# A convolution by Fourier transforms with its gradients: the inverse transforms' first step over halves of the array's rows, and state sums of two exponents at a time

## The chip, the core and the metric

The kernel runs on one core of a Trainium2 chip. The core has TensorE (PE, matrix products; PEld in the profile is its loading of weights), VectorE (DVE), ScalarE (ACT), GpSimd (POOL) and SyncE (SP, which here only issues DMAs). The engines run side by side, each works through its own queue in order, and semaphores tie them together. Products are written to PSUM, from which VectorE or ScalarE must copy them to SBUF; such a copy is called an evacuation below. The metric is the device time of one execution in microseconds, lower is better.

## What is computed

A layer's forward pass and all its gradients. The forward pass, cut to its core:

```python
xn = layernorm(x)                                    # 2048 rows of 512 channels, bf16
P  = exp(dt*A * l)                                   # per channel 128 complex states, l = 0..2047
K  = real(einsum("dn,dnl,dn->dl", C, P, dt*B))       # one convolution kernel per channel
s  = irfft(rfft(xn, 4096) * rfft(K, 4096))[:2048] + xn * Dskip
g  = silu(silu(xn @ w1) @ w2)                        # w1 512 x 1792, w2 1792 x 512
out = x + s * g
```

Beside `out` the kernel returns the gradients of x, A, B, C (real and imaginary parts), log_dt, Dskip, w1 and w2 for a given gradient of `out`.

## The kernel before

**Transforms.** A transform of 4096 points is done by products with small tables, in blocks of 128 channels. Forward (`dft_fwd`): a first step with the table TF (L405), transposes (L415), and a second step with F2 (L425); F2 has 64 columns, and its products are written alternately to the lower and the upper 64 PSUM partitions. Inverse (`dft_inv`): a first step with the spectrum Y as the stationary operand and the table I2 as the moving one (L440), then a second with TI (L453). In the first step there are 16 groups of 128 spectrum rows, and each group takes a product for the real and one for the imaginary part, 128 rows by 256 columns, both added into the same part of PSUM. Four groups are one set: eight products, then one evacuation (the `ev` call behind them), which sorts the values into A2. A set fills two PSUM banks. I2 holds a twiddle table times a mask: row p of a group meets only those 8 of the 128 columns' places that belong to it, and the mask is built in `gen_step_tables` from the row's number (`pg`, `e8`). There are 12 inverse transforms: one for each of four blocks in the forward convolution (stream C, `gen_conv_fwd`), two for each block in the backward one (stream B, `gen_conv_bwd`).

**State gradients.** The kernel's gradient is folded (`gen_ssm_fold`) and multiplied by the powers of the state matrix (`gen_ssm_v`, L998, evacuated to Vb). VectorE multiplies Vb with the table E (`gen_ssm_products`, L1013, to Tp): real and imaginary products for each of 21 exponents. `gen_ssm_sums` adds them up over the exponents on TensorE, by products with the identity matrix, in the PSUM tile psS: three rows of 64 values a partition. It does so for 16 groups, four for each block of channels; ScalarE copies each group's psS into Sa (L1037). `gen_ssm_grads` starts by subtracting the third row of Sa from the first (L1072), and goes on to the parameters' gradients.

**Order.** All instructions are issued in an order written out by hand or by a planner. Every part of the work is a generator, and every `yield` ends a step. PLAN is a string with a letter for each step: `play` takes the letters in order and advances the named generator. PLAN has seven sections, parted by `/`; between them memory pools are closed and opened. Since each engine's queue is in order, PLAN is the order of every queue, SP's and POOL's DMAs included. WAYS says for each evacuation of a stream whether ScalarE (A) or VectorE (D) does it. SLOTS says which buffer of a rotating set each tile takes. Streams named below: 0 to 8 and p are the setup (7 the magnitudes, ScalarE exponentials at L508; 6 the layer norm; 5 the step tables); J, F the forward dense pass (L751, L768); P, Q, R the tables and the convolution kernels; X, C the forward convolution; D, B the backward one; d, A, x the backward dense pass (L1149, L1169); N, Y, V, T, S, Z the state gradients; h, t, w and g, v the gradients of the dense weights (L1202, L1231); i, k, m the layer norm's gradient.

Section 2 of PLAN (counted from 1) holds the forward convolution with the forward dense pass, section 4 the backward convolution with the backward dense pass, section 5 the state gradients' start with the last of the backward dense pass, section 6 the state gradients with the dense weights' gradients.

Of the kernel before, what the change touches and what calls it, by code (L numbers as in the profile page):

```python
# [39 lines left out]
AAAAAAYAAAAAANNxVVVVAAxVVVVVVAATTVVxxVVxVVYxVVTYYxxxxNNNTTTTNSVVVVVVVYxSx/VTTSTSVTTVVVVVhhVVVSSVVVVVVVTTTYYttTtSthVTTNTT  # L40
tttYwwtSVVVVSgVVVVtStthVtNNwNNwNVTwTTVVVwwNNNNZZTgStZSZZVtVVwVZtZtYYYhgvvYvvVZTTTTVVwVwZZVZVVSVVVVVYtTSTTTVvvwVttVVSVVVV
TTTvSTwgVVVhVVSYvtZZttwYYTTVThTVZtVVvZvZtVVVVVTSvvhVVVVSVVtSwwVVvVwTTTTwtTYYYVVVVZSSVTVVVZTTYtZZttZtvtVVVSVtTSVVVVvvVTgT
TZYZYTTwTVVVZZwvVVVZVZZVZhwwwSwStghtVVggVVSStwZgvVVZZVVhTTTvZZZTvTvTTSvvTvtSSStttvgthZvvwwttZZttZgZwwwZhZZZZvZvZZtttwwt/
wttivtiikkhvkwwikktkmkkmkkkmttmmmkimmvgkvvviigvvvvvwwkkmvttvkkkkwwvvkmkwkgmwwwkkimmkkmkmvmkmmmvvvvvvvvvmvkkkkmmmvmvvvvvv
# [5 lines left out]
fp.XT=01010101;pf.pf=012010210210210210210210210210210210210210210120120120120120121210210120120120120201202102102102102  # L50
102102102102102021020202012012021020210212012010120120120120202012012012012012012012012012020102121021021021021201201201
2012012010101020120101202;fp.hT=0101010101010101;fp.ob=0101010;dft.w8=01231032013123032120132021032103;pc.pc=01010101010
101010101010101010101010101010101010101010101010101010101001010101011010101010101010110101010101010101010101010101010101
010101010101010101010101010101010101010101010101010101010101010101010101010101010101010101010101010101010101010101010101
010101001;tbl.tv=01011101010110100010101010010101;tbl.ts=01010101110100101010101000101010;tbl.W=01010101010010101010;dft
.t4=0101001010101010;gate.g=01234567;gate.S=01;da.doT=01010101;da.dhT8=01201201;da.dhT6=01010101;dftb.w8b=0101;go.go_s=0
1010101;go.go_r=010101;go.go_g=01010101;go.go_x=01201201;da.pd_s=0101010101010101;sb.YT=0101010101010101;sb.Eb=01010101;
sb.Gf=0101;sb.Gb=01010101;sb.Vb=0101010101010101;sb.Tp=0101010101010101;sb.Sa=0101;fw.h_in=01010101010101;fw.a_tok=01010
# [6 lines left out]
WAYS = """J=DAAAADDD;  # L65
F=AADAAAAAAAAADAAADAAAAAAAAAAADDAAAAAAADADAAAADAAADAAAAAAAADDAADADDDDDDDAA;
X=AAAADAAAAAAAAADAAAAAAAAAADAAAAAAAAAAAAAD;
R=AAAAAAADAADDADAAAAAAAAAAAAAAAADDDDDDDDAADAAADAAAAADDAAAAADAAAAAADAAAAAAADAAAADDA;
C=AADDAAAAAAAAAAAAAAAADDAAAAAAADAAADAAADAAAAADDADAADADDDADAAAAAAAA;
W=DDDDADDDDDDDDD;  # L70
D=AAAADDAAAADAAAAAAAAAAAAAADAAAADAADAAAAAA;
d=DDADAAAA;
B=AADAADAAAAAADAAAAAAAAAAAAAAAAAADDADAAADAAAAAAAAAAAAAADDA;
x=ADADAAADDADADDAA;
V=ADDADDADADDADADAAAAAAADDAAAAADAAADAAAAAAAAAAADAAAAAAAAAAAAAAADAA;
w=DADDDDAAAAAAAA;
v=DADADDDAADDAAAAAAAAADAAADAAA"""
# [82 lines left out]
def setup_tiles(k, wp):  # L160
# [13 lines left out]
    for nm, q in (("c8", [16, 8]), ("c4", [16, 4]), ("e8", [16, 8]), ("e4", [16, 4]), ("ia", [4]), ("kf", [2, 64]), ("kk", [128])):  # L174
        new(nm, q, I32)
    new("mask", [128])
    new("maskf", [64])
    new("kq", [3, 128], I32)
    new("sf", [2, 64])
    new("sv", [3, 128])  # L180
    for nm in ("p_t", "p_h", "p_e", "p_g", "pj"):
        new(nm, [1], I32)
# [19 lines left out]
    for nm, shape, dt in (("rstd", [k.T], F32), ("xn", [k.T, D], BF16), ("ident", [P], BF16), ("zero", [P], BF16), ("onesf", [1], F32),  # L202
                          ("pi", [1], F32), ("mpi", [1], F32), ("ecst", [NE + len(Y_EXP)], F32), ("TF", [16, 2, 128], BF16),
                          ("TI", [32, 128], BF16), ("F2", [2, 64], BF16), ("I2", [2, 2, 128], BF16), ("FO", [4, 128], BF16), ("MK", [2, NE, 4], BF16)):
        setattr(k, nm, c.tile([P] + shape, dt, name=nm))
# [7 lines left out]
def gen_plain_consts(k, w):  # L213
# [16 lines left out]
    for nm, q in (("c8", [[1, 16], [0, 8]]), ("c4", [[1, 16], [0, 4]]), ("e8", [[0, 16], [1, 8]]), ("e4", [[0, 16], [1, 4]])):  # L230
        G.iota(getattr(w, nm)[:], pattern=q, base=0, channel_multiplier=0)
# [59 lines left out]
def gen_step_tables(k, w):  # L291
# [4 lines left out]
    c8, c4, e8, e4 = w.c8, w.c4, w.e8, w.e4  # L296
    ip = w.ip
    pt, ph, pe, pg, sh, kf, kk, mask, maskf, kq, sf, sv, pj, pa, m4, rl = (
        getattr(w, nm) for nm in "p_t p_h p_e p_g sh kf kk mask maskf kq sf sv pj pa m4 rl".split())
# [4 lines left out]
    nc.vector.scalar_tensor_tensor(out=pg[:], in0=ph[:], scalar=4.0, in1=pe[:], op0=ALU.mult, op1=ALU.add)  # L304
# [8 lines left out]
    TT(out=kk[:], in0=flat(c8), in1=pt[:].to_broadcast([P, 128]), op=ALU.mult)  # L313
    TT(out=mask[:], in0=flat(e8), in1=pg[:].to_broadcast([P, 128]), op=ALU.is_equal)
# [10 lines left out]
    TT(out=sv[:], in0=sv[:], in1=mask[:].unsqueeze(1).to_broadcast([P, 3, 128]), op=ALU.mult)  # L325
# [107 lines left out]
def dft_inv(k, A2, Y, ev, prepare, consume):  # L433

    nc, pc = k.nc, k.pc
    for g0 in range(0, 16, 4):
        ps = pc.tile([P, 4, 32, 8], F32, name="ps_i2", tag="pc")
        for g in range(4):
            for c in range(2):
                nc.tensor.matmul(out=ps[:, g], lhsT=Y[:, c, g0 + g, :], rhs=k.I2[:, c].rearrange("p c m -> p (c m)"),  # L440
                                 start=(c == 0), stop=(c == 1))
        yield
        ev(A2[:].rearrange("p c t (g e) -> p g (c t) e", e=8)[:, g0:g0 + 4], ps[:])
        yield
    for h in range(2):
        if prepare:
            prepare(8 * h, 8)
            yield
        ps = pc.tile([P, 8, P], F32, name="ps_i1", tag="pc")
        for j in range(8):  # L450
            t = 8 * h + j
            for c in range(2):
                nc.tensor.matmul(out=ps[:, j], lhsT=k.TI[:, 2 * t + c, :], rhs=A2[:, c, t, :], start=(c == 0), stop=(c == 1))  # L453
        yield
        consume(8 * h, 8, ps)
        yield
# [564 lines left out]
def gen_ssm_sums(k, sb, groups):  # L1021
# [3 lines left out]
    for i, (b, h, q0) in enumerate(groups):  # L1025
        Tp = k.Tp.pop(i)
        if i % 4 == 0:
            Sa = sb.tile([P, 3, 32, 2, 4], F32, name="Sa", tag="Sa", bufs=2)
        psS = k.pt.tile([P, 3, 64], F32, name="psS", tag="pt")
        for e in range(NE):  # L1030
            nc.tensor.matmul(out=psS[:, 0:2], lhsT=k.ident[:], rhs=flat(Tp[:, 0, e]), start=(e == 0), stop=False)
        for r in range(2):
            nc.tensor.matmul(out=psS[:, 1 + r:2 + r], lhsT=k.ident[:], rhs=flat(Tp[:, 1, 0, r:r + 1]), start=False, stop=False)
        for e in range(1, NE):
            nc.tensor.matmul(out=psS[:, 1:3], lhsT=k.ident[:], rhs=flat(Tp[:, 1, e]), start=False, stop=(e == NE - 1))
        yield
        nc.scalar.copy(out=Sa[:, :, 16 * h + q0:16 * h + q0 + 8], in_=psS[:].rearrange("p r (q w a) -> p r q w a", w=2, a=4))  # L1037
# [5 lines left out]
def gen_ssm_grads(k, b, sb):  # L1043
# [27 lines left out]
    w_ = lambda t: v(t[:])  # L1071
    TT(out=S[:, 0], in0=S[:, 0], in1=S[:, 2], op=ALU.subtract)  # L1072
# [372 lines left out]
```

## Time and profile before

| | us |
|---|---|
| median of 3 runs | 607.57 (607.13 to 607.59) |
| the profiled execution, device time | 606.76 |
| its span, first to last instruction | 605.0 |
| mean granted TensorE clock | 0.989 of full |

The page of the profile has the busy time of each engine over the span. The same by stages of the run comes from the view of windows. The timeline lists instructions in order of time and merges neighbours of one line: start, length from the first's start to the last's end, line, output and inputs, shape (stationary rows*columns, then moving operand), and how many. A matmul's length holds its way through the pipeline, which overlaps with the next one; the distance between two starts tells what it takes in a stream. The view of groups has for each line and shape the count, the busy time, the mean of one in ns and the idle time of the engine before them.

### The profile page before, as it was taken

Reading aid. Unit: us, or ns where it says so; the run is one execution under the profiler, and the core shown is the slowest. Engines: PE = TensorE matmul, PEld = TensorE weight load, DVE = VectorE, ACT = ScalarE, POOL = GpSimd, SP = SyncE. Lnnn points to the kernel's source line nnn. Section 1 sums busy time; section 2 is a strip of 40 time slices with the busy share of each in tenths; the row PEclk is TensorE's granted clock in tenths of the full one; section 3 lists DMA queues with packets and bytes.
Section 4 is the critical chain, followed back from the end, with each engine's and each line's share of the span. In section 5 each row is a group of like instructions: output and inputs, shape, how many; then the busy total and the mean of one; then the engine's idle time right before and its main releaser. Section 6 shows DMA issues by size and latency. Waiting matters only on the chain. (4 is left out here: it accounts for less than half of the span.)

```text
span 605.0 us, 14383 instructions
## 1 busy us (share of the span) xinstructions
PE 560.1 (93%) x5861; PEld 425.3 (70%) x5884; DVE 533.0 (88%) x906; ACT 443.2 (73%) x552; POOL 77.5 (13%) x171
## 2 busy tenths in 40 slices
PE   1597989999999989999999999999799999999995
PEld 1354758677777686786787767775787888795864
DVE  8989999999999889999998799568759889978894
ACT  7989989999998669998787864641575456434661
POOL 6211001010101120000000100000000202123121
PEclk9988999999999999999999999999999999999998
DMA  9896678676658598959877798797999999999993
GB/s 267 260 306 203 254 245 287 225 249 236 248 160 331 216 297 322 330 126 294 276 232 250 233 296 253 210 230 181 242 202 207 232 252 150 246 207 270 309 242 132
DMA packets 156066, 146.83 MB, mean 243 GB/s; under 512 B 79520, under 2 KB 133024, under 8 KB 152416
## 3 DMA queue, kind: packets, MB, share of 16 engines
q1 hardware_dynamic: 146688, 123.10, 72.1%
q0 software_dynamic: 6768, 19.93, 9.2%
q10 hardware_dynamic: 2544, 2.88, 1.5%
q8 instruction: 46, 0.75, 0.5%
q14 instruction: 20, 0.16, 0.1%
HBM read 63.44 MB, written 62.00 MB: 207 GB/s over the span
## 5 line engine op out<-in xcount | busy, mean ns | idle before, releaser
L112 ACT CAST dA<-ps_s 128x1024 bf16<-128x1024 f32 x86 | 86.3, 1037 | 7.6 <-PE ps_s L425 4.0
L751 PE MATMUL ps_h<-XT,W 128*128 128x256 bf16 x448 | 57.4, 279 | 6.2 <-ACT hT L112 4.6
L112 ACT CAST Vb<-ps_v 128x672 bf16<-128x672 f32 x49 | 34.1, 723 | 37.3 <-PE ps_v L998 32.7
L1149 PE MATMUL ps_da<-doT,W 128*128 128x256 bf16 x448 | 55.2, 273 | 1.2 <-ACT pd_s L112 1.1
L1013 DVE TENSOR_TENSOR Tp<-Vb,Eb 128x1344 bf16<-128x1344 bf16 x64 | 51.0, 850 | 5.9 <-ACT Vb L112 5.9
L768 PE MATMUL ps_o<-W,aT 128*128 128x512 bf16 x214 | 52.7, 399 | 1.1 <-issue 0.9
L112 ACT CAST dB<-ps_i 128x1024 bf16<-128x1024 f32 x41 | 41.1, 1031 | 16.4 <-PE ps_i L440 15.6
L751 PEld LDWEIGHTS <-W 128*128 128x128 bf16 x448 | 43.6, 100 | 12.9 <-issue 7.3
L1231 PE MATMUL ps_w<-dh_tok,xn 128*128 128x256 bf16 x448 | 51.8, 273 | 0.1
L1169 PE MATMUL ps_dx<-W,dhT 128*128 128x512 bf16 x224 | 50.8, 379 | 0.0
L1202 PE MATMUL ps_w<-YD,a_tok 128*128 128x512 bf16 x214 | 49.8, 379 | 0.5
L440 PE MATMUL ps_i<-I,sp_in 128*128 128x256 bf16 x384 | 47.3, 273 | 1.7 <-ACT dB L112 1.7
L1149 PEld LDWEIGHTS <-W 128*128 128x128 bf16 x448 | 42.8, 98 | 8.0 <-issue 2.8
L1231 PEld LDWEIGHTS <-xn 128*128 128x128 bf16 x448 | 43.2, 98 | 5.9 <-issue 0.5
L1152 DVE TENSOR_TENSOR dhT<-ps_da,dhT 128x512 bf16<-128x512 f32 x56 | 37.2, 684 | 10.3 <-PE ps_da L1149 7.3
L440 PEld LDWEIGHTS <-sp_in 128*128 128x128 bf16 x384 | 37.0, 98 | 8.9 <-DVE dB L113 1.9
L768 PEld LDWEIGHTS <-aT 128*128 128x128 bf16 x224 | 22.0, 102 | 29.3 <-issue 7.9
L1169 PEld LDWEIGHTS <-dhT 128*128 128x128 bf16 x224 | 21.3, 98 | 24.2 <-issue 1.2
L1202 PEld LDWEIGHTS <-a_tok 128*128 128x128 bf16 x224 | 21.5, 98 | 23.2
L466 DVE TENSOR_TENSOR cm<-sp_in,dA 128x2048 bf16<-128x2048 bf16 x24 | 29.3, 1219 | 4.9 <-DMA sp_in<-KXd 3.3
L425 PE MATMUL ps_s<-dB,F 128*64 128x512 bf16 x192 | 28.2, 388 | 3.8 <-ACT dB L112 2.1
L571 ACT ACTIVATE sn<-V 128x2048 bf16<-128x2048 int16 (+1 forms) x16 | 30.5, 1905 | 1.1 <-DVE V L567 1.1
(241 smaller groups left out, 1254.2 us busy)
## 6 DMA issues: line engine op xcount, KB each, us to landing
Yd<-YD SPq DMA_DIRECT2D x8, 1024.0 KB, 4.9
sp_in<-Ud SPq DMA_DIRECT2D x8, 1024.0 KB, 7.3
h_in<-Hd SPq DMA_DIRECT2D x14, 512.0 KB, 5.1
Ed<-E SPq DMA_DIRECT2D x8, 672.0 KB, 3.9
Eb<-Ed SPq DMA_DIRECT2D x8, 672.0 KB, 5.4
Hd<-hT POOLq DMA_DIRECT2D x8, 512.0 KB, 6.1
Ud<-dA SPq DMA_DIRECT2D x4, 1024.0 KB, 5.2
KXd<-dA SPq DMA_DIRECT2D x4, 1024.0 KB, 4.3
```

The source lines that it names most:

```text
L112: return self.nc.scalar.copy(out=out, in_=in_)
L440: nc.tensor.matmul(out=ps[:, g], lhsT=Y[:, c, g0 + g, :], rhs=k.I2[:, c].rearrange("p c m -> p (c m)"), start=(c == 0), stop=(c == 1))
L466: TT(out=t2[:], in0=b[:, :, gs], in1=a[:, 1:2, gs].to_broadcast([P, 2, n, P]), op=ALU.mult)
L571: nc.scalar.activation(out=sn[:, 0:n], in_=low, func=ACT.Sin, scale=-2 * PI_LO / 2.0 ** PB)
L751: nc.tensor.matmul(out=ps[:, j], lhsT=k.W1[:, dk, ft * P:ft * P + P], rhs=XTv[:, :, dk, :], start=(dk == 0), stop=(dk == DK - 1))
L768: nc.tensor.matmul(out=ps[:], lhsT=aT[:, ft, t * P:t * P + P], rhs=k.W2[:, ft, :], start=(ft == 0), stop=(ft == FT - 1))
L1013: k.nc.vector.tensor_tensor(out=Tp[:, c, :, r ^ c].rearrange("p e (q w) a -> p q w e a", w=2), in0=Vb[:, :, c].rearrange("p q w (e a) -> p ...
L1149: nc.tensor.matmul(out=ps[:, j], lhsT=k.W2[:, ft, dk * P:dk * P + P], rhs=dTv[:, :, dk, :], start=(dk == 0), stop=(dk == DK - 1))
L1152: nc.vector.tensor_tensor(out=dh[:, i0:i0 + 2, :], in0=ps[:], in1=dh[:, i0:i0 + 2, :], op=ALU.mult)
L1169: nc.tensor.matmul(out=ps[:], lhsT=dhs[ft // 8][:, ft % 8, t * P:t * P + P], rhs=k.W1[:, :, ft * P:ft * P + P], start=(ft == 0), stop=(ft ...
L1202: nc.tensor.matmul(out=ps[:], lhsT=at[:, t, :], rhs=k.do[:, t, :], start=(t == 0), stop=(t == k.T - 1))
L1231: nc.tensor.matmul(out=ps[:], lhsT=k.xn[:, t, dk * P:dk * P + P], rhs=dh[:, t].rearrange("p j n -> p (j n)"), start=(t == 0), stop=(t == k ...
```

## The change

In `dft_inv` each product of the first step is split by rows: rows 0 to 63 and rows 64 to 127 of Y are separate stationary operands, each with the matching half of I2, and each half is written to its own PSUM bank (index z). A half's rows belong to four of the eight places, so I2 has 64 places in each part where it had 128. A set is now 16 products of 64 rows by 128 columns. The evacuation writes the same values to the same places of A2, in runs of four elements. The tables' setup loses `c8`, `e8`, `mask` and `p_g`.

In `gen_ssm_sums` one product with the identity takes two exponents (256 columns), the even and the odd one into separate halves of psS; the 21st stands alone. The copy to Sa has 384 values a partition in place of 192, and `gen_ssm_grads` first adds the two halves.

PLAN, SLOTS and WAYS are written anew throughout. The number of steps of each stream is the same. Cut to its core:

```diff
 def dft_inv
     for g0 in range(0, 16, 4):
-        ps = pc.tile([P, 4, 32, 8], F32, name="ps_i2", tag="pc")
+        ps = pc.tile([P, 2, 4, 32, 4], F32, name="ps_i2", tag="pc")
         for g in range(4):
             for c in range(2):
-                nc.tensor.matmul(out=ps[:, g], lhsT=Y[:, c, g0 + g, :], rhs=k.I2[:, c].rearrange("p c m -> p (c m)"),
-                                 start=(c == 0), stop=(c == 1))
+                for z in range(2):
+                    zs = slice(64 * z, 64 * z + 64)
+                    nc.tensor.matmul(out=ps[:, z, g], lhsT=Y[zs, c, g0 + g, :], rhs=k.I2[zs, c].rearrange("p c m -> p (c m)"),
+                                     start=(c == 0), stop=(c == 1))
         yield
-        ev(A2[:].rearrange("p c t (g e) -> p g (c t) e", e=8)[:, g0:g0 + 4], ps[:])
+        ev(A2[:].rearrange("p c t (g z e) -> p g z (c t) e", z=2, e=4)[:, g0:g0 + 4].rearrange("p g z x e -> p z g x e"), ps[:])
...
 def gen_ssm_sums
-        psS = k.pt.tile([P, 3, 64], F32, name="psS", tag="pt")
-        for e in range(NE):
-            nc.tensor.matmul(out=psS[:, 0:2], lhsT=k.ident[:], rhs=flat(Tp[:, 0, e]), start=(e == 0), stop=False)
+        psS = k.pt.tile([P, 2, 3, 64], F32, name="psS", tag="pt")
+
+        def add(z, r0, r1, rhs, first=False, last=False):
+            out = psS[:, 0:z, r0:r1].rearrange("p z r x -> p z (r x)")
+            nc.tensor.matmul(out=out, lhsT=k.ident[:], rhs=rhs.rearrange("p z r x a -> p z (r x a)"), start=first, stop=last)
+        for e in range(0, NE, 2):
+            n = min(2, NE - e)
+            add(n, 0, 2, Tp[:, 0, e:e + n], first=e == 0)
         for r in range(2):
-            nc.tensor.matmul(out=psS[:, 1 + r:2 + r], lhsT=k.ident[:], rhs=flat(Tp[:, 1, 0, r:r + 1]), start=False, stop=False)
-        for e in range(1, NE):
-            nc.tensor.matmul(out=psS[:, 1:3], lhsT=k.ident[:], rhs=flat(Tp[:, 1, e]), start=False, stop=(e == NE - 1))
+            add(2, 1 + r, 2 + r, Tp[:, 1, 0:2, r:r + 1])
+        for e in range(2, NE, 2):
+            n = min(2, NE - e)
+            add(n, 1, 3, Tp[:, 1, e:e + n], last=e + 2 >= NE)
...
 def gen_ssm_grads
+    TT(out=S[:, 0], in0=S[:, 0], in1=S[:, 1], op=ALU.add)
+    S = S[:, 0]
     TT(out=S[:, 0], in0=S[:, 0], in1=S[:, 2], op=ALU.subtract)
...
 def gen_step_tables
-    nc.vector.scalar_tensor_tensor(out=pg[:], in0=ph[:], scalar=4.0, in1=pe[:], op0=ALU.mult, op1=ALU.add)
...
-    TT(out=kk[:], in0=flat(c8), in1=pt[:].to_broadcast([P, 128]), op=ALU.mult)
-    TT(out=mask[:], in0=flat(e8), in1=pg[:].to_broadcast([P, 128]), op=ALU.is_equal)
+    TT(out=kk[:], in0=flat(c4), in1=pt[:].to_broadcast([P, 64]), op=ALU.mult)
...
-    TT(out=sv[:], in0=sv[:], in1=mask[:].unsqueeze(1).to_broadcast([P, 3, 128]), op=ALU.mult)
+    TT(out=sv[:], in0=sv[:], in1=maskf[:].unsqueeze(1).to_broadcast([P, 3, 64]), op=ALU.mult)
```

Evacuations by VectorE, of all of a stream, before and after:

| stream | J | F | R | C | W | d | B | x | V | w | v |
|---|---|---|---|---|---|---|---|---|---|---|---|
| all | 8 | 72 | 80 | 64 | 14 | 8 | 56 | 16 | 64 | 14 | 28 |
| VectorE before | 4 | 19 | 21 | 15 | 13 | 3 | 9 | 7 | 15 | 5 | 9 |
| VectorE after | 5 | 17 | 24 | 16 | 14 | 5 | 8 | 4 | 13 | 2 | 8 |

Section 4 of PLAN takes one step of A and two each of x, d and s more than before, mostly from section 5.

More of the change, by code (lines that the diff above doesn't have):

```diff
@@ new lines @@
+RRPQQPRQQQQQQQQFFFFRFRRRFXQXFFFFFXFRRXJPPRRRRPPPXXRRXRRFXQXRXXRFFQXXQRQRRRRRPQQQRQQPFXPXXQQRRCFFFFXFPCPPFFRCFCRFFCCFFJRR
+RCCRFCQFQFQFQFUFFFFRRCFCCCFFRCPQCCCRFCFFCQQCQQQQCRRRRPPPCFFXFXXXRRRCCRCFCCFFFFCCCCRJRCFXRRQQFFQFFQQXXRXRFFQQFQCUCCCFRPQQ
+PFXXXPRRRRXFRQXXXRRRPJJRXXRXCCRRPCPPFCCXCXFRRRPQQPCQCCFCFFXQRQJPPFQFCFFCCFCFFXXFFFRRRRQFCQQQFFFFFCCRCCCQJCRRCCRCCCRRCCCJ
+CRQFFCCPXRFXRRQXXXQXRRCCCXRXRQQRQQRRRQXQXXFXFRRRFXXCPPFQXRCXCFRFCCPPFFCPPXQFXRURRFFFXRCCUFFFFCQQCRQFQRQFFCCCCFCCQQRCCCQR
+RRFFQCCRRCCFRRRRCCRRCCCRQRCCCRCCCCRFRFFCCCRRRCCCCRCRRFF/CCCCFFCCGGGCCFFCCCCCCGGGGGGLGGGFCFCFFFFCCFFFFCCGGFFGGGGCGCCCCCGG
@@ new lines @@
+FGCFCCCHHCCCCHCGGCFFCCCWCWWWWCWCCHGCCWWGWGWHHHHWWCCCCWDWWWDDDWDWWDWDWWWDWWWMMDCDDLDDDLLDLDDMDMWMWD/DdDdDEadsEDdADDDAADBB
+DAAaasaaAAAADBBBDDDsAAAAABBooooBBBAAAAABAAABoBBDDAoBBBBABBBsAoBABBBBEoEDDDxDBBDAADBlBAAsxxBBAABxBOOOxoBBBBdBDDxxllllDDDB
+BBBaaBBdxDxxxOOBBBOOOAlBaBBBBAADDdOBdBBBBBoBoAAoDDsBBODBAooODAoAoAADDBBABABBAAAEBBsaBBBOAAAAADOOOBOADDBDoBoBBOBxAOAODBDD
+xDDsAAADDDDDoBoBoABAABBAABxBBOodOOOoOoDoODOOdOdOsOdxDxEDxBBBAAAABBAooBBBDoADDBDADDAxDDBBBaBOaBBEAxOoBBxBABBxAOxsBBsBABAA
+AxBBBEBAAaoBBABBABxxBBBAABBBABBBxxBsxBBABBBBOBBBBABBBOOaaaABxBBxAABBBAABAAsAABBBBBddddxxsA/NYxAAAAAAsNNNNYYxaNAAxYxAAAVA
@@ L61 @@
 """.replace("\n", "").split(";") if x)
-WAYS = """J=DAAAADDD;
-F=AADAAAAAAAAADAAADAAAAAAAAAAADDAAAAAAADADAAAADAAADAAAAAAAADDAADADDDDDDDAA;
+WAYS = """J=DAAADDDD;
+F=AADAAAAAAADADAAADAAAAAAAAAAAAAAAAAAAADADDAAADAAADAAAAAAAADDAAAADDDDADDAA;
 X=AAAADAAAAAAAAADAAAAAAAAAADAAAAAAAAAAAAAD;
[L68 to L77, printed above, removed]
+R=AAAAAAADDADDAADAAAAAAAAAAAAAAADDDDDDDDAAAADADAAAAAADAADDAAAADAAADADAAAADDADAAAAA;
+C=AADDAAAAAAAAAAAAAAAADDAAAAAAADAAADAAADAAAAADDADAADDDDDDAAAAAAAAA;
+W=DDDDDDDDDDDDDD;
+D=AAAADDAAAADAAAAAAAADAAAAADAAAAAAAADAAAAA;
+d=DDDAADDA;
+B=AAAAAAAAAAADAAADAAAAAAAADAAAAAAADAADAAADAAAAAAAAAAAADADA;
+x=DADAAAAAADADAAAA;
+V=ADAAAAAADDDDAAAAAAADDDDAAADADAAAAAAAAAAAAAAAAAAAAADADAAAAAAAAAAA;
+w=AADAAAAAADAAAA;
+v=DDDDAAADAADADDAAAAAAAAAAAAAA"""
 class Placed:
@@ L173, in setup_tiles @@
     new("ip", [4], I32)
-    for nm, q in (("c8", [16, 8]), ("c4", [16, 4]), ("e8", [16, 8]), ("e4", [16, 4]), ("ia", [4]), ("kf", [2, 64]), ("kk", [128])):
+    for nm, q in (("c4", [16, 4]), ("e4", [16, 4]), ("ia", [4]), ("kf", [2, 64]), ("kk", [64])):
         new(nm, q, I32)
-    new("mask", [128])
     new("maskf", [64])
-    new("kq", [3, 128], I32)
+    new("kq", [3, 64], I32)
     new("sf", [2, 64])
-    new("sv", [3, 128])
-    for nm in ("p_t", "p_h", "p_e", "p_g", "pj"):
+    new("sv", [3, 64])
+    for nm in ("p_t", "p_h", "p_e", "pj"):
         new(nm, [1], I32)
@@ L229, in gen_plain_consts @@
     G.iota(w.ip[:], pattern=[[0, 4]], base=0, channel_multiplier=1)
-    for nm, q in (("c8", [[1, 16], [0, 8]]), ("c4", [[1, 16], [0, 4]]), ("e8", [[0, 16], [1, 8]]), ("e4", [[0, 16], [1, 4]])):
+    for nm, q in (("c4", [[1, 16], [0, 4]]), ("e4", [[0, 16], [1, 4]])):
         G.iota(getattr(w, nm)[:], pattern=q, base=0, channel_multiplier=0)
@@ L295, in gen_step_tables @@
     flat = lambda t: t[:].rearrange("p a b -> p (a b)")
-    c8, c4, e8, e4 = w.c8, w.c4, w.e8, w.e4
+    c4, e4 = w.c4, w.e4
     ip = w.ip
-    pt, ph, pe, pg, sh, kf, kk, mask, maskf, kq, sf, sv, pj, pa, m4, rl = (
-        getattr(w, nm) for nm in "p_t p_h p_e p_g sh kf kk mask maskf kq sf sv pj pa m4 rl".split())
+    pt, ph, pe, sh, kf, kk, maskf, kq, sf, sv, pj, pa, m4, rl = (
+        getattr(w, nm) for nm in "p_t p_h p_e sh kf kk maskf kq sf sv pj pa m4 rl".split())
     TS(out=pt[:], in_=ip[:, 0:1], scalar=2, op=ALU.arith_shift_right)
@@ L1027, in gen_ssm_sums @@
         if i % 4 == 0:
-            Sa = sb.tile([P, 3, 32, 2, 4], F32, name="Sa", tag="Sa", bufs=2)
-        psS = k.pt.tile([P, 3, 64], F32, name="psS", tag="pt")
-        for e in range(NE):
-            nc.tensor.matmul(out=psS[:, 0:2], lhsT=k.ident[:], rhs=flat(Tp[:, 0, e]), start=(e == 0), stop=False)
+            Sa = sb.tile([P, 2, 3, 32, 2, 4], F32, name="Sa", tag="Sa", bufs=2)
+        psS = k.pt.tile([P, 2, 3, 64], F32, name="psS", tag="pt")
[5 more added lines that the diff above has]
+            add(n, 0, 2, Tp[:, 0, e:e + n], first=e == 0)
         for r in range(2):
-            nc.tensor.matmul(out=psS[:, 1 + r:2 + r], lhsT=k.ident[:], rhs=flat(Tp[:, 1, 0, r:r + 1]), start=False, stop=False)
-        for e in range(1, NE):
-            nc.tensor.matmul(out=psS[:, 1:3], lhsT=k.ident[:], rhs=flat(Tp[:, 1, e]), start=False, stop=(e == NE - 1))
+            add(2, 1 + r, 2 + r, Tp[:, 1, 0:2, r:r + 1])
+        for e in range(2, NE, 2):
+            n = min(2, NE - e)
+            add(n, 1, 3, Tp[:, 1, e:e + n], last=e + 2 >= NE)
         yield
-        nc.scalar.copy(out=Sa[:, :, 16 * h + q0:16 * h + q0 + 8], in_=psS[:].rearrange("p r (q w a) -> p r q w a", w=2, a=4))
+        nc.scalar.copy(out=Sa[:, :, :, 16 * h + q0:16 * h + q0 + 8].rearrange("p z r q w a -> p (z r) q (w a)"),
+                       in_=psS[:].rearrange("p z r (q x) -> p (z r) q x", q=8))
         if i % 4 == 3:
```

44 lines of the change are left out of this document (17 added, 27 removed).

## The prediction

> **What bounds the kernel now.** I read the page first, then the busy time by stage, then the instructions of one backward stretch on TensorE.
>
> ```profile
> span 605.0 us, 14383 instructions
> PE 560.1 (93%) x5861; PEld 425.3 (70%) x5884; DVE 533.0 (88%) x906; ACT 443.2 (73%) x552; POOL 77.5 (13%) x171
> ```
>
> ```profile
> 0.00:60.00 60.00, 35.70 (x258) 23.55 (x262) 54.23 (x127) 54.26 (x71) 18.33 (x73) 0.91 0.86 259
> 60.00:255.00 195.00, 186.97 (x2187) 141.67 (x2195) 186.87 (x249) 178.36 (x223) 21.26 (x30) 1.00 0.74 263
> 255.00:405.00 150.00, 148.42 (x1412) 112.55 (x1410) 127.14 (x166) 110.84 (x110) 6.53 (x12) 1.00 0.81 241
> 405.00:440.00 35.00, 31.10 (x332) 23.12 (x330) 27.84 (x34) 12.18 (x18) 0.00 (x0) 1.00 0.83 199
> 440.00:600.00 160.00, 157.92 (x1683) 124.44 (x1690) 136.94 (x333) 87.52 (x133) 31.36 (x56) 1.00 0.99 230
> ```
>
> The columns after the length are PE, PEld, DVE, ACT, POOL, the granted clock, the DMA share and GB/s. Up to 60 us VectorE and ScalarE are the fuller ones. From 60 to 255 us three engines are full together: PE 187.0, DVE 186.9, ACT 178.4 of 195. From 255 to 405 us (backward convolutions with the dense backward pass) TensorE alone is full, 148.4 of 150, while DVE has 22.9 us to spare. From 440 us PE is full again, 157.9 of 160, with the DMA share at 0.99. So a product saved between 255 and 405 us, or after 440, should shorten the run by nearly what it costs; one saved between 60 and 255 us need not.
>
> Busy time overstates a matmul, since its 0.2 us of pipeline is counted. What one costs in a stream is the distance of starts:
>
> ```profile
> 295.74 1.67 PE L1169 MATMUL ps_dx<-W,dhT 128*128 128x512 bf16 x7
> 297.25 0.61 PE L405 MATMUL ps_s<-ds,TF 128*128 128x128 bf16 x8
> 297.70 1.04 PE L440 MATMUL ps_i<-I,sp_in 128*128 128x256 bf16 x8
> 298.57 1.04 PE L1149 MATMUL ps_da<-doT,W 128*128 128x256 bf16 x8
> 299.44 1.91 PE L440 MATMUL ps_i<-I,sp_in 128*128 128x256 bf16 x16
> ...
> 305.62 1.91 PE L1149 MATMUL ps_da<-doT,W 128*128 128x256 bf16 x16
> 307.36 1.95 PE L415 MATMUL pt_f<-ident,dA 128*128 128x128 bf16 x32
> 309.15 1.91 PE L1149 MATMUL ps_da<-doT,W 128*128 128x256 bf16 x16
> 310.99 0.62 PE L425 MATMUL ps_s<-dB,F 128*64 128x512 bf16 x4
> 311.54 1.05 PE L440 MATMUL ps_i<-I,sp_in 128*128 128x256 bf16 x8
> ```
>
> Seven products of 512 columns take 297.25 - 295.74 = 1.51 us, 0.216 each; eight of 256 take 0.87, 0.109 each; eight of 128 take 0.45, 0.056 each. Time goes by columns: one of 256 costs hardly less than two of 128. Weight loads are hidden, and stay hidden at 84 columns:
>
> ```profile
> 120.34 0.73 PEld L639 LDWEIGHTS <-YD 128*128 128x128 bf16 x16
> 120.45 0.77 PE L639 MATMUL ps_k<-W,YD 128*128 128x84 bf16 x16
> 121.05 1.03 PE L751 MATMUL ps_h<-XT,W 128*128 128x256 bf16 x8
> ```
>
> Sixteen loads and products in 0.60 us, 0.037 a pair.
>
> **Part 1: the first step over halves of the rows.** There are 12 inverse transforms with four sets each, 48 sets of L440. A set is eight products of 256 columns now, 0.87 us. It becomes 16 products of 64 rows and 128 columns: eight pairs, whose two members use different halves of the rows and write different PSUM banks.
>
> ```profile
> 60.00:255.00 195.00, 15.77 (x128) 12.43 (x128) 1.00 0.74 263
> 255.00:405.00 150.00, 31.57 (x256) 24.60 (x256) 1.00 0.81 241
> ```
>
> These are L440's rows by stage (PE, PEld): 16 sets before 255 us, 32 after, in the stage where PE alone is full.
>
> No run here has products of 64 rows. Bounds for a pair: not under 0.056, since each member streams 128 columns; 0.112 if they run one after the other. The nearest row is L425, whose products use one half of the columns each, alternately: four of 512 columns pass in 311.54 - 310.99 = 0.55 us, where one after the other they would need 4 x 0.216 = 0.86. They run two by two. I take 0.056, so 0.45 us a set and 0.42 saved.
>
> The same row shows a price. Two pairs would need 0.43, so 0.12 is lost inside and on leaving; and the 16 products of L1149 before it take 310.99 - 309.15 = 1.84 where 16 take 307.36 - 305.62 = 1.74, so 0.10 is lost on entering. A visit to the divided array costs 0.22. Its bounds for rows are 0 (no such pause) and 0.42, at which a set gains nothing. I take 0.22. In the new order 16 of the 48 sets follow another with no other product between (found by walking its letters with the generators' yields), so there are 32 visits: 21 between 255 and 405 us, 11 before.
>
> 255 to 405 us: 32 x 0.42 - 21 x 0.22 = 13.4 - 4.6 = **8.8 us saved**. VectorE, at 127.1, can follow: the stage would be 141 long. Before 255 us: 16 x 0.42 - 11 x 0.22 = 4.3 us of PE, with DVE and ACT nearly as full as PE. Between 0 and 4.3 I take **1.0**.
>
> The evacuation of a set writes runs of four elements, not eight. That costs nothing: half of the dA below is written in runs of four already.
>
> ```profile
> L112 ACT CAST dA<-ps_s 128x1024 bf16<-128x1024 f32 x86 | 86.3, 1037 | 7.6 <-PE ps_s L425 4.0
> L112 ACT CAST dB<-ps_i 128x1024 bf16<-128x1024 f32 x41 | 41.1, 1031 | 16.4 <-PE ps_i L440 15.6
> ```
>
> ACT's 15.6 us of waiting for L440 can only get shorter by sets that finish earlier.
>
> [...]
>
> **Part 2: state sums.**
>
> ```profile
> 480.25 1.34 PE L1031 MATMUL psS<-Tp,ident 128*128 128x128 bf16 x21
> 481.43 0.22 PE L1033 MATMUL psS<-Tp,ident 128*128 128x64 bf16 x2
> 481.48 1.28 PE L1035 MATMUL psS<-Tp,ident 128*128 128x128 bf16 x20
> 482.60 0.74 PE L998 MATMUL ps_v<-Gb,YT 128*128 128x168 bf16 x8
> ```
>
> A group is 43 products in 2.35 us. It becomes 19 of 256 columns and 4 of 128: 19 x 0.109 + 4 x 0.056 = 2.29. The columns stay, so 16 groups save 16 x 0.06 = **0.9 us**. Added: ScalarE copies 384 values instead of 192, and VectorE adds the halves, 768 values, four times. Neither size is in the trace:
>
> ```profile
> L1037 ACT COPY Sa<-psS 128x192 f32<-128x192 f32 x16 | 5.2, 326 | 16.0 <-PE psS L1035 16.0
> L112 ACT CAST KE<-ps_e 128x448 bf16<-128x448 f32 x4 | 2.3, 585 | 0.0
> L1072 DVE TENSOR_TENSOR Sa<-Sa 128x256 f32<-128x256 f32 x4 | 1.7, 415 | 2.3 <-ACT Sa L1037 2.3
> L564 DVE TENSOR_TENSOR V<-tau,ecst 128x1024 int32<-128x1024 f32 x8 | 9.7, 1217 | 0.0
> ```
>
> The copy lies between 0.33 and 0.59, by length about 0.52: 16 x 0.2 = 3 us of ACT, which is idle 72 us after 440. The add lies between 0.42 and 1.22, by length about 0.95: 3.8 us of DVE, which is idle 23 us there, and WAYS moves six evacuations of the streams V, w and v from DVE to ACT. Each stands in front of products Tp on DVE's queue that PE's sums wait for; without that cover it would cost up to 3.8. I take 0.
>
> **Part 3: setup and order.** Two iotas on POOL and two DVE instructions (p_g, mask) go, and others halve.
>
> ```profile
> 4.17 0.45 DVE L314 TENSOR_TENSOR mask<-e,p_g 128x128 f32<-128x128 int32 x1
> 5.36 0.63 DVE L318 TENSOR_SCALAR kq<-kq 128x384 int32<-128x384 int32 x1
> 8.88 0.52 DVE L325 TENSOR_TENSOR sv<-sv,mask 128x384 f32<-128x384 f32 x1
> ```
>
> 0.45 and about half of the other two is 1.0 us ahead of the first normalised rows; between 0 and 1.0 I take **0.5**. No DMA is added; the loads of x move ahead of the weights on SP's queue. The new order finishes one or two tiles' worth of A and x (8 products of 256, 14 of 512: 0.9 and 3.0 us) before the state gradients start instead of beside their start at 405 to 440, where they fill PE's wait for the first products. The work is the same, but up to 3.9 us of idle can open there. I take **1.0 lost**.
>
> Sum: 606.76 (the profiled execution, 605.0 of it span) - 8.8 - 1.0 - 0.9 - 0.5 + 1.0 = 596.6. That execution is 0.8 under the median of 607.57, so **597.4 us**. Its own range, with the front at 0 to 4.3 and the refill at 0 to 3.9, is 593 to 601.3.
>
> **Rivals.** *The halves run one after the other* (slower). A set takes 16 x 0.056 = 0.90 and each visit still 0.22: 48 x 0.03 + 32 x 0.22 = 8.5 us more PE, 5.6 of it where PE alone is full. With half of the rest and all else as above, 607.6 + 5.6 + 1.4 - 0.9 - 0.5 + 1.0 = 614.2. It decides from a pair of 0.091 upward, where 21 visits eat what 32 sets save. Against it stands L425; for it, that row halves add into two banks of the same partitions at once, which no row shows.
>
> *Each pair exposes its weight loads.* The first products of a visit to L425 are longer than the rest:
>
> ```profile
> L425 PE MATMUL ps_s<-dB,F x192: 376/379/403, 50.3 to 350.3; 128*64 128x512 bf16 x192
> ```
>
> 403 - 379 = 24 ns. At every pair that makes 0.080 and 0.64 a set: 32 x 0.23 - 4.6 = 2.8 saved, 1.0 lost to the refill, 0.9 and 0.5 gained, 0.3 in front: 604. For it: two loads per 0.056 us is 0.028 each, less than the 0.037 shown. [...] Against: L425's second pairs are back at 379.
>
> *The start slips.* The new order has 30 steps of the magnitudes ahead of the first dense product, now 22.
>
> ```profile
> 8.48 11.02 ACT L508 ACTIVATE mag_all<-lamr 128x512 bf16<-128x512 f32 x21
> 19.41 0.56 ACT L112 CAST hT<-ps_h 128x512 bf16<-128x512 f32 x1
> ```
>
> At 11.02 / 21 = 0.52 each that is 8 x 0.52 = 4.2 us later for the first hT, so 597.4 + 4.2 = 601.6. Against it: the exponentials have to be done anyway and ACT is full up to 255 us in either order.
>
> **Chances.** Forecast 0.55, exposed loads 0.15 (604), late start 0.12 (601.6), one after the other 0.13 (614.2), anything else 0.05. About 0.2%, 1.2 us, is what a measurement of this kernel can tell from no change. Faster: 0.55 + 0.12 + most of 0.15, so 0.80; within 0.2%: 0.04; slower: 0.16. The range for 8 in 10 is 591 to 610: its low end is the full 4.3 us in front and 1.0 in setup with no refill, 592.6, and some pauses shorter than 0.22; its high end takes in the exposed loads and leaves out most of the slower case.
>
> **What would show it.** Right: L440's successor twice as many products with starts in pairs a few ns apart, a set of 0.45 us, 0.1 us of gap on each side; the stage up to the last backward inverse some 8 us shorter with PE still full; a sum group of 2.29 us; four DVE adds of 0.95. Wrong: starts of the halves 0.056 apart; pairs of 0.080; PE idle opening in the state gradients' start; a stage that keeps its length with DVE or ACT full in PE's place.

## The result, and the profile after

| | before | after |
|---|---|---|
| median, us | 607.35 (606.13 to 607.59, 4 runs) | 599.39 (597.31 to 601.44, 4 runs) |
| profiled execution, us | 606.76 | 598.29 |
| its span, us | 605.0 | 596.5 |

The ratio is 0.9861, 95% interval 0.9829 to 0.9894: 8 us less, 1.4%.

From the page of the changed kernel, span and busy times:

```profile
span 596.5 us, 14501 instructions
PE 545.3 (91%) x5920; PEld 404.5 (68%) x5948; DVE 532.3 (89%) x904; ACT 446.7 (75%) x556; POOL 77.4 (13%) x169
```

TensorE has lost 14.8 us of busy time, and the span fell by 8.5. Where the time went is read from the first and last starts of four lines, in the view of one tile's instructions (count, shortest/median/longest in ns, first and last start, shape). Of the kernel before:

```profile
L1149 PE MATMUL ps_da<-doT,W x448: 269/273/282, 255.6 to 410.8; 128*128 128x256 bf16 x150
L453 PE MATMUL ps_i<-dB,TI x384: 216/219/229, 137.6 to 385.3; 128*128 128x128 bf16 x192
L1031 PE MATMUL psS<-Tp,ident x336: 217/219/219, 424.1 to 541.1; 128*128 128x128 bf16 x168
L1231 PE MATMUL ps_w<-dh_tok,xn x448: 269/273/283, 465.6 to 598.3; 128*128 128x256 bf16 x150
```

Of the changed kernel, the same products under their new line numbers:

```profile
L1157 PE MATMUL ps_da<-doT,W x448: 269/273/283, 257.7 to 402.0; 128*128 128x256 bf16 x150
L452 PE MATMUL ps_i<-dB,TI x384: 216/219/230, 138.9 to 379.7; 128*128 128x128 bf16 x192
L1032 PE MATMUL psS<-Tp,ident x368: 219/272/273, 417.1 to 533.9; 128*128 128x256 bf16 x152, 128*128 128x128 bf16 x32
L1239 PE MATMUL ps_w<-dh_tok,xn x448: 270/273/283, 456.3 to 590.6; 128*128 128x256 bf16 x150
```

These starts cut the span into five stretches: the **front**, to the first product of the dense backward pass; the **backward** stretch, on to the last inverse transform; the **refill**, to the first state sum; the **gradients**, to the last product of the dense weights' gradients; and the tail.

| us | front | backward | refill | gradients | tail | span |
|---|---|---|---|---|---|---|
| before | 255.6 | 129.7 | 38.8 | 174.2 | 6.7 | 605.0 |
| after | 257.7 | 122.0 | 37.4 | 173.5 | 5.9 | 596.5 |
| difference | +2.1 | -7.7 | -1.4 | -0.7 | -0.8 | -8.5 |

Nearly all of the gain is in the backward stretch. Its busy times before and after, in the view of windows (length, PE, PEld, DVE, ACT, POOL, clock, DMA share, GB/s):

```profile
255.60:385.30 129.70, 129.32 (x1248) 98.23 (x1246) 118.28 (x153) 98.00 (x99) 6.53 (x12) 1.00 0.78 241
```

```profile
257.70:379.70 122.00, 119.62 (x1503) 86.78 (x1501) 116.44 (x152) 99.14 (x101) 6.53 (x12) 1.00 0.84 264
```

PE was busy for all but 0.4 us of it and is now idle for 2.4; DVE has gone from 91% to 95% of it. What a set of the first step takes is read from TensorE's timeline of the changed kernel (start, length, line, output and inputs, shape, count):

```profile
283.75 0.60 PE L1157 MATMUL ps_da<-doT,W 128*128 128x256 bf16 x4
284.28 1.07 PE L439 MATMUL ps_i<-I,sp_in 64*128 64x128 bf16 x32
285.28 3.20 PE L1177 MATMUL ps_dx<-W,dhT 128*128 128x512 bf16 x14
...
299.02 1.05 PE L1157 MATMUL ps_da<-doT,W 128*128 128x256 bf16 x8
300.00 0.62 PE L439 MATMUL ps_i<-I,sp_in 64*128 64x128 bf16 x16
301.31 0.62 PE L439 MATMUL ps_i<-I,sp_in 64*128 64x128 bf16 x16 [0.69 <-DVE dB L113]
301.87 1.05 PE L1157 MATMUL ps_da<-doT,W 128*128 128x256 bf16 x8
```

Two sets in a row take 285.28 - 284.28 = 1.00 us, one alone 301.87 - 301.31 = 0.56: a set is 0.44, and 0.12 goes on a visit's first products and on leaving. Entering costs 284.28 - 283.75 - 4 x 0.109 = 0.09 and 300.00 - 299.02 - 8 x 0.109 = 0.11. These are the 0.45 and the 0.22 of the prediction. Inside the visit at 284.28 the products start in pairs: 284.346 and .349, .402 and .405, .458 and .461. The evacuation in runs of four costs nothing that shows: the casts dB<-ps_i take 1046 ns on ScalarE (1031 before) and 1218 on VectorE in both kernels.

### The profile page after: what moved, and what is told of

Same layout as the page of the kernel before. It is cut to its first block, busy times and chain, and to the rows that moved or that the text cites. A ratio compares the mean times of both kernels' runs of the same rounds, so it can differ in the third digit from the quotient of the medians.

```text
span 596.5 us, 14501 instructions
## 1 busy us (share of the span) xinstructions
PE 545.3 (91%) x5920; PEld 404.5 (68%) x5948; DVE 532.3 (89%) x904; ACT 446.7 (75%) x556; POOL 77.4 (13%) x169
## 4 chain that ended last, share of the span: by engine, by line
DVE 38%; PE 36%; ACT 12%; issue 5%; DMA 5%; SPq 2%; DVEq 0%; ACTq 0%
PE ps_da L1157 6%; PE ps_dx L1177 5%; PE ps_w L1239 5%; PE ps_w L1210 3%; DVE cm L465 3%; PE psS L1032 3%; ACT mag_all L507 3%; DVE sp_in L467 3%; DVE Tp L1012 3%; ACT dA L112 2%; DVE W L632 2%; PE ps_o L767 2%; DMA YD<-Od 2%; DVE dB L113 2%; PE pt_t L134 2%
## 5 line engine op out<-in xcount | busy, mean ns | idle before, releaser
L750 PEld LDWEIGHTS <-W 128*128 128x128 bf16 x448 | 43.1, 100 | 13.9 <-issue 7.7
L112 ACT CAST Vb<-ps_v 128x672 bf16<-128x672 f32 x51 | 35.3, 727 | 19.2 <-PE ps_v L997 12.2
L112 ACT CAST dB<-ps_i 128x1024 bf16<-128x1024 f32 x40 | 40.7, 1046 | 11.8 <-PE ps_i L439 11.6
L1157 PEld LDWEIGHTS <-W 128*128 128x128 bf16 x448 | 41.7, 98 | 8.8 <-issue 2.4
L1032 PE MATMUL psS<-Tp,ident 128*128 128x256 bf16 (+1 forms) x368 | 39.4, 263 | 0.0
L1032 PEld LDWEIGHTS <-ident 128*128 128x128 bf16 x368 | 33.6, 98 | 3.3
```

Source lines behind the costliest of these rows:

```text
L112: return self.nc.scalar.copy(out=out, in_=in_)
L750: nc.tensor.matmul(out=ps[:, j], lhsT=k.W1[:, dk, ft * P:ft * P + P], rhs=XTv[:, :, dk, :], start=(dk == 0), stop=(dk == DK - 1))
L1032: nc.tensor.matmul(out=out, lhsT=k.ident[:], rhs=rhs.rearrange("p z r x a -> p z (r x a)"), start=first, stop=last)
L1157: nc.tensor.matmul(out=ps[:, j], lhsT=k.W2[:, ft, dk * P:dk * P + P], rhs=dTv[:, :, dk, :], start=(dk == 0), stop=(dk == DK - 1))
```

## The experiments

The kernel before ran beside every group of runs, and its median was 607.35, 609.52, 608.85 and 608.92 us in the four comparisons, so kernels of different groups are compared by their ratio to it. The stretches are those of the profiled execution, read as above.

| kernel | ratio (95%) | front | backward | refill | gradients | span |
|---|---|---|---|---|---|---|
| before | 1 | 255.6 | 129.7 | 38.8 | 174.2 | 605.0 |
| after | 0.9861 (0.9829 to 0.9894) | 257.7 | 122.0 | 37.4 | 173.5 | 596.5 |
| after_again | 0.9867 (0.9839 to 0.9895) | 259.8 | 121.9 | 37.6 | 173.2 | 598.4 |
| after_third | 0.9846 (0.9822 to 0.9870) | 258.1 | 122.5 | 37.3 | 173.5 | 597.3 |
| whole_new_order | 0.9972 (0.9946 to 0.9997) | 260.5 | 129.0 | 37.2 | 173.2 | 605.9 |
| halves_old_order | 0.9950 (0.9923 to 0.9978) | 257.6 | 127.8 | 38.2 | 174.2 | 604.5 |
| halves_in_turn | 0.9917 (0.9896 to 0.9938) | 260.1 | 125.7 | 37.2 | 173.2 | 602.2 |
| sums_old_order | 1.0015 (0.9997 to 1.0033) | 258.3 | 129.2 | 39.2 | 175.0 | 608.4 |
| single_sums_new_order | 0.9811 (0.9782 to 0.9841) | 258.7 | 121.9 | 37.7 | 172.4 | 596.6 |
| single_sums_again | 0.9828 (0.9810 to 0.9847) | 257.5 | 122.1 | 37.3 | 173.2 | 596.1 |
| pairs_no_add | 0.9825 (0.9805 to 0.9844) | 258.7 | 122.0 | 37.5 | 171.7 | 595.9 |
| add_on_pool | 0.9925 (0.9907 to 0.9943) | 257.6 | 122.6 | 37.3 | 178.1 | 601.6 |
| old_front_single_sums | 0.9815 (0.9790 to 0.9839) | 256.2 | 121.9 | 37.9 | 172.5 | 594.5 |
| old_front_again | 0.9805 (0.9787 to 0.9823) | 257.2 | 122.1 | 37.5 | 174.1 | 596.8 |

The table has its own yardsticks. Up to 255 us sums_old_order has the same instructions in the same order as the kernel before, and its front is 258.3 against 255.6; the changed kernel's own front came out at 257.7, 259.8 and 258.1. So a difference of less than 3 us between two single fronts means nothing. The gradients' stretch is steadier with the paired sums in the new order (173.2 to 173.5 in five profiles with the add on VectorE), less so with single sums there (172.4 to 174.1 in four).

**The changed kernel again.**

> The changed kernel once more, for its time beside the other kernels of the same chip: 597 to 602 us, as its four runs so far (597.3 to 601.4). A set of L439 takes 0.45 us and a visit to the divided array 0.21.

> The changed kernel a third time, for a comparison on one chip with the next three: ratio to the kernel before 0.985 to 0.989.

Measured: 601.53 and 599.11 us, ratios 0.9867 and 0.9846. The first is as expected; the second ratio lies just under the 0.985 expected.

**Halves or order?** Two kernels part the change. In the first, the halves go, with their tables and their evacuation, and the order and the paired sums stay (the diff is cut to the products):

```diff
-                for z in range(2):
-                    zs = slice(64 * z, 64 * z + 64)
-                    nc.tensor.matmul(out=ps[:, z, g], lhsT=Y[zs, c, g0 + g, :], rhs=k.I2[zs, c].rearrange("p c m -> p (c m)"),
+                nc.tensor.matmul(out=ps[:, g], lhsT=Y[:, c, g0 + g, :], rhs=k.I2[:, c].rearrange("p c m -> p (c m)"),
```

> The changed kernel with the inverse transforms' first step over whole rows again; new order and paired sums stay. If the halves save TensorE time (theory): a set is 0.87 us again in place of 0.45, without 0.21 for a visit, so 32 x 0.42 - 21 x 0.21 = 9 us come back in the backward stage and 0 to 4 before it: 607 to 612 us. If the new order is what made the kernel faster (rival): within 2 us of the changed kernel, 597 to 602.

In the second, the kernel before gets `dft_inv` and the tables of the changed one, and keeps its PLAN, SLOTS, WAYS and sums:

> The kernel before with the halves alone; old order and old sums. Theory: old order has 31 visits, 20 of them in the backward stage, so 32 x 0.42 - 20 x 0.21 = 9 us of TensorE time go there and the other engines, with 20 us to spare, follow in the old order too: 597 to 600 us. If the order matters (rival): 604 to 608, because each queue still waits in the old places.

Measured: 607.71 us for the first, at the low end of what the theory expected; the halves are worth 601.53 - 607.71 = -6.2 us in the new order. The second came to 606.50, against the theory's 597 to 600 and as the rival had it. Neither half of the change makes 8 us alone: the order (with the paired sums) gives 0.3% in whole_new_order, the halves 0.5% in halves_old_order, all of it 1.4%. The backward stretch tells why. With whole rows in the new order, and with halves in the old one:

```profile
260.50:389.50 129.00, 128.49 (x1247) 98.71 (x1245) 117.84 (x152) 99.27 (x101) 6.56 (x12) 1.00 0.80 251
```

```profile
257.60:385.40 127.80, 121.43 (x1503) 87.49 (x1501) 118.03 (x153) 97.54 (x99) 6.54 (x12) 1.00 0.78 244
```

In the old order PE's busy time falls by 7.9 us (from 129.32), but the stretch by 1.9 only. What took the place of the saved products is in PE's waits in that stretch of halves_old_order (who waits for whom, us in total, times, longest):

```profile
PE ps_da L1148 <- DVE doT L113: 0.9, 1, 0.9
PE ps_da L1148 <- DVE dhT L1151: 0.9, 1, 0.9
PE pt_t L134 <- DVE YD L871: 0.8, 1, 0.8
PE ps_i L439 <- DVE sp_in L471: 0.7, 2, 0.4
PE ps_i L439 <- DVE sp_in L469: 0.7, 1, 0.7
PE ps_i L452 <- ACT dB L112: 0.6, 1, 0.6
PE ps_da L1148 <- ACT pd_s L112: 0.5, 1, 0.5
```

These are the seven longest, together 5.1 of the 6.4 us that PE idles there: seven different operands come late, none by a full us. In the kernel before, the same view has one wait of 0.3 us. The likely reading is that each queue was in step with a slower TensorE, and a faster one runs into all of them a little. Fewer visits are not what the new order brings: the old one makes 20 to the divided array in this stretch, the new one 21. PLAN, SLOTS and WAYS were changed together, and no run shows which of them does it. The new order, with whole rows, leaves the stretch at 129.0: there it had nothing to gain. It gains 6.9 us from the halves (129.0 to 122.1, the mean of three). Between the profiles with the order held, whole_new_order and the changed kernel, PE's busy time in the stretch falls by 8.9 us (128.49 to 119.62) and its idle time grows from 0.5 to 2.4.

**Do the halves run side by side?** The same products, loads and banks, one half after the other:

```diff
-        for g in range(4):
-            for c in range(2):
-                for z in range(2):
+        for z in range(2):
+            for g in range(4):
+                for c in range(2):
```

> The changed kernel with the loop over halves outermost: all eight products of rows 0 to 63, then the eight of rows 64 to 127; the same products, loads and banks. Theory (two halves save time because they run side by side): only one pair of a set can overlap, a set takes 16 x 0.056 = 0.9 us in place of 0.45, 14 us more in the backward stage and 0 to 7 before it: 614 to 622 us. Rival (it is the smaller products or the order that save): within 3 us of the changed kernel.

Measured: 603.45 us, ratio 0.9917; 3 to 4 us slower than the changed kernel by the ratios (3.6 in the backward stretch, 125.7 to 122.1), and 10 us under the low end of what the theory expected. TensorE's timeline of this kernel:

```profile
285.85 0.86 PE L439 MATMUL ps_i<-I,sp_in 64*128 64x128 bf16 x16
286.64 1.05 PE L1157 MATMUL ps_da<-doT,W 128*128 128x256 bf16 x8
287.62 1.34 PE L439 MATMUL ps_i<-I,sp_in 64*128 64x128 bf16 x32
288.90 3.20 PE L1177 MATMUL ps_dx<-W,dhT 128*128 128x512 bf16 x14
```

A set takes 0.79 us alone where the changed one takes 0.56, not the 1.02 that 16 x 0.056 and the visit's 0.12 would make. The single starts, from the trace, in us:

```
285.848 .914 .970 286.025 .081 .090 .137 .157 .193 .213 .249 .269 .325 .380 .436 .492
```

Five products 0.056 apart, then three pairs, then five alone. Read as two rows 0.056 apart, eight begin at .848 (to .249) and eight at .090 (to .492): the second half's first product starts ahead of the first half's last three. The semaphores on the records bear this reading out where a second set follows at once: in the visit at 287.62 the record that carries the second set's wait, which stands on its first product, starts at 288.105, and the one that carries the first set's signal to the evacuation, which stands on its last product and is queued ahead, at 288.265. It is so in 14 visits of this kernel and in none of the changed one. So halves did overlap here even where they are queued one after the other, and queueing them alternately gave twice that overlap (of that 1.02 us a set alone saves 0.23 here and 0.46 where the halves alternate). The theory stands, that time is saved by running side by side; the size I expected rested on my estimate that only one pair of a set overlaps.

**What do the paired sums cost?** Four kernels: single sums in the changed kernel (`gen_ssm_sums` and the add of the kernel before), the paired sums alone in the kernel before, and the changed kernel without the add, or with the add on GpSimd.

```diff
-    TT(out=S[:, 0], in0=S[:, 0], in1=S[:, 1], op=ALU.add)                        # pairs_no_add
+    nc.gpsimd.tensor_tensor(out=S[:, 0], in0=S[:, 0], in1=S[:, 1], op=ALU.add)   # add_on_pool
```

> The changed kernel with one exponent a product again in the state sums, halves and new order as changed. Theory: a group of sums takes 2.35 us in place of 2.29, 0.9 in all, and the four adds of 0.95 and the longer copies that go were hidden: 599 to 601. Rival (adds and copies stand in VectorE's and ScalarE's way): 3 us less than the changed kernel, 595 to 597.

> Single sums in the new order once more. If the paired sums cost 3 us or more, as the first medians had it: 3 to 4 us less than after_third, ratio near 0.981. If about 1 us, as the first profiles' stages had it (173.3 in place of 172.4 us from the first sum to the last dense gradient): ratio 0.984 to 0.987.

> The kernel before with the paired sums alone, old order. By the prediction: 0.9 us less than the kernel before, adds and copies hidden. Rival (the add on VectorE and the longer copy delay what the sums and the dense gradients wait for): up to 4 us more than the kernel before, as single_sums_new_order (3.9 us less than the changed kernel beside it) suggests.

> The changed kernel without the add of the two halves of the sums: the state gradients are worked out from the first half alone. If the four adds of 0.95 us on VectorE are what the paired sums cost: about 3 us less than the changed kernel, as single_sums_new_order. If the longer copies or the order of the queue cost it, or nothing does and the difference was the runs' spread: as the changed kernel within 1.5 us.

> The changed kernel with the four adds of the sums' halves on GpSimd in place of VectorE. If the add costs time because it stands on VectorE ahead of other work: 1.5 to 2.5 us less than the changed kernel, as pairs_no_add, ratio 0.981 to 0.985. If what costs is that the state gradients behind it begin later: as the changed kernel or a little slower.

The view of groups of the changed kernel has the added work in the sizes forecast, 0.48 us for a copy (0.52) and 0.95 for an add (0.95):

```profile
L1042 ACT COPY Sa<-psS 128x384 f32<-128x384 f32 x16 | 7.7, 479 | 20.2 <-PE psS L1032 20.2
L1078 DVE TENSOR_TENSOR Sa<-Sa 128x768 f32<-128x768 f32 x4 | 3.8, 950 | 3.3 <-ACT Sa L1042 3.3
```

On TensorE a group of 43 products took 2.35 us (480.25 to 482.60 in the prediction's lines) and one of 23 takes 2.29:

```profile
480.78 2.46 PE L1032 MATMUL psS<-Tp,ident 128*128 128x256 bf16 x23
483.07 0.74 PE L997 MATMUL ps_v<-Gb,YT 128*128 128x168 bf16 x8
```

By the single starts it is 2.348 and 2.298, 0.05 us for 20 products fewer: 2.5 ns each, and 0.8 us for the 16 groups. That part of the forecast holds. Against it stand the copies and adds. Single sums came out 3.9 us under the changed kernel in the first comparison (597.62 to 601.53) and 0.4 in the second (598.71 to 599.11); the first lies between the theory's 599 and the rival's 597, the second ratio, 0.9828, between its two cases. In the old order the paired sums made 0.9 us more by the ratio (interval -0.2 to 2.0), where 0.9 less was forecast. Without the add the changed kernel's ratio is 0.9825, some 2 us less, where 3 was expected if the adds are the cost. So no run shows a saving, and all the medians lie on one side; how large the cost is, between 0.4 and 4 us, these runs leave open. The gradients' stretch does not settle it: with single sums it is 172.4, 173.2, 172.5 and 174.1, with the paired ones 173.2 to 173.5. It says more of the add alone, since without it the stretch is shorter than in every other profile of the new order:

```profile
L1032 PE MATMUL psS<-Tp,ident x368: 219/272/273, 418.2 to 533.7; 128*128 128x256 bf16 x152, 128*128 128x128 bf16 x32
L1238 PE MATMUL ps_w<-dh_tok,xn x448: 269/273/283, 457.0 to 589.9; 128*128 128x256 bf16 x150
```

589.9 - 418.2 = 171.7, 1.7 us less than the 173.4 of the changed kernel's three. By this one profile about 2 of the 3.8 us of adds are hidden and the rest is not.

The add on GpSimd was the wrong cure: 0.9925, and 604.70 us against the 599.11 of the changed kernel beside it, slower than either case expected. Its group and VectorE's next instruction:

```profile
L1078 POOL TENSOR_TENSOR Sa<-Sa 128x768 f32<-128x768 f32 x4 | 7.2, 1812 | 15.4 <-ACT Sa L1042 15.4
L1080 DVE TENSOR_TENSOR Sa<-Sa 128x256 f32<-128x256 f32 x4 | 1.7, 425 | 11.2 <-POOL Sa L1078 11.2
```

GpSimd needs 1.81 us for it, and the subtraction behind it still stands in VectorE's queue: VectorE now idles 11.2 us in four waits, with the products Tp behind it. The gradients' stretch grew by 4.7 us, to 178.1.

**The front.** The old order up to the backward convolutions, with its buffers and ways, the new order behind, halves throughout and single sums (in outline; the sections of PLAN are numbered from 0 here):

```diff
-PLAN = new[0] / new[1] / new[2] / new[3] / ...
+PLAN = old[0] / old[1] / old[2] / "DD" + new[3] / ...
```

> Halves everywhere, single sums, with the old order up to the backward convolutions (sections 1 to 3 of PLAN, with their buffers and ways) and the new order behind. If the new order of the front costs time (the first backward dense product starts at 255.6 us in the kernel before, at 257.7 to 260.5 in those with the new order): 2 to 4 us less than single_sums_new_order beside the same kernel before, a ratio near 0.976. Rival (the difference is the spread of the runs, or the halves disturb the old front too, as 257.6 in halves_old_order suggests): ratio 0.980 to 0.985.

> Halves, single sums, old order up to the backward convolutions, once more. If the old front is worth 2 us, as its profile shows (first backward dense product at 256.2 in place of 258.7 us): 2 us less than single_sums_again. If its first run's median holds: equal to it within 1 us.

597.07 and 597.12 us, ratios 0.9815 and 0.9805, against 0.9811 and 0.9828 for single sums with the new front. The first ratio is in the rival's range. The second kernel ran beside single_sums_again and is 1.6 us less, where 2 or none was expected; the intervals overlap. The fronts of the profiled executions are 256.2 and 257.2 against 258.7 and 257.5, within the spread. By the ratios both runs are under all three of the changed kernel; that the old front is worth 1 to 2 us is possible and not shown.

## Why the prediction was right, and where not

- **The size of a set and of a visit** (0.45 and 0.22 us): right, read off the rows of the 64-column products (L425), which divide the array by columns and not by rows. The rival that each pair exposes its weight loads, and the one of one half after the other, fell: pairs start 0.056 apart. Half the columns are enough for a half of the rows because the mask leaves each row one of the eight places, 16 of the 128 columns (not 8, as the text ahead of the prediction has it), and rows 0 to 63 use places 0 to 3.
- **8.8 us in the backward stretch**: 7.7 between the two kernels, 6.9 with the order held. The mechanism was right: TensorE's work was what bounded the stretch, and its busy time fell by 8.9 with the order held. The size was a little large, since 2 us of that became waits, and a condition was missing. That VectorE "can follow" was read from busy time alone. In the old order PE waited for late operands and 1.9 us came of the halves; most of the gain needed the new order, which I had costed only for what it moves.
- **1.0 us before 255 us, and 0.5 of setup**: the front got 2.1 us longer between the two profiles, not 1.5 shorter, but equal instructions differ by 2.7 there (255.6 and 258.3), so no run shows what the halves are worth in front: 260.5 with whole rows in the new order against 257.5 to 259.8 in seven profiles with alternating halves, 256.2 to 257.6 in three with halves in the old one. The start is steady. The smaller tables bring the first dense product 0.3 us forward in the old order (13.60 in the kernel before, 13.28 in halves_old_order) and 1.2 in the new one (16.95 in whole_new_order, 15.76), where the forecast was 0.5. The new order's front starts later all the same, in part as the rival said. The first dense product of the changed kernel and of the one with the old front (old_front_again):

```profile
L750 PE MATMUL ps_h<-XT,W x448: 269/273/421, 15.8 to 223.4; 128*128 128x256 bf16 x150
```

```profile
L750 PE MATMUL ps_h<-XT,W x448: 269/273/421, 13.3 to 226.1; 128*128 128x256 bf16 x150
```

  It starts 2.5 us later. The rival had 4.2 for the first evacuation, hT. On ScalarE, behind the exponentials, the first one starts at 22.97 us, against 19.41 in the kernel before, 3.6 later; but VectorE now takes one at 21.02, so the first of all is 1.6 later. How much of this is left at the backward stretch is not shown.
- **0.9 us saved by the sums, adds and copies at 0**: very likely wrong in sign. TensorE saves 0.8 us, but single sums came out faster in both comparisons in the new order, and no run shows a gain. The step that failed is the cover of the adds at 0: without them the stretch is 1.7 us shorter. That VectorE "is idle 23 us there" is a sum over a stretch, and the add has a fixed place in a queue, ahead of the products Tp; that this is what cost the 1.7 is argued, not shown.
- **1.0 us lost in the refill**: wrong in sign, 1.4 gained (38.8 to 37.4). The forecast was that idle time opens on PE; instead PE's idle time there went from 1.8 us (37.05 busy of 38.80) to 0.1 (37.33 of 37.40). It is the new order's doing: 37.2 with whole rows in the new order, 38.2 with halves in the old one.
- **The sum**: 597.4 forecast, 599.39 measured. The errors in the front (3.6 too good), the backward stretch (1.1 too good) and the refill (2.4 too bad) partly cancel. That the total came within 2 us is in part luck; that the gain lies in the backward stretch and comes from the halves is not.

## What to carry to other kernels

A product over the full 128 rows whose upper and lower 64 rows feed different outputs can be cut into row halves in separate PSUM banks; queued alternately they took half the time here (0.44 us a set for 0.87). Put such sets together, since each visit to the divided array cost 0.2 us here, half a set's gain. When one engine's work shrinks in a kernel with a fixed order, count on little until the order is made anew: here the old order gave 3 us, the new one 8 in all. Merging matmuls at the same number of columns saved only 2.5 ns each, so the instruction that it adds elsewhere has to be free, and an engine's idle time over a stretch does not show that it is.

## What the runs showed of the hardware that was not expected

In halves_in_turn products of the second row half start before products of the first half that are queued ahead of them. By the pattern of the starts in the trace the second half's first product starts 0.047 us before the first half's sixth (286.090 and 286.137); by the semaphores on the records the first product of the next set starts 0.160 us before the last one of the set ahead of it (288.105 and 288.265). So for these products of that run the starts do not keep the order of the queue, as the text ahead of the prediction takes every engine's to do. In the changed kernel the same two records keep it: in the visit at 284.28 the last product of the first set starts at 284.684, the first of the second at 284.737. On GpSimd an add of 128 x 768 f32 took 1.81 us, on VectorE 0.95.
